# Two orders of one hand-written table of steps: packed attention and a gated feed-forward layer on one core

## The chip, the core and the metric

The kernel runs on one core of a Trainium2 chip. The metric is the device time of one execution in microseconds (us); lower is better. The time of the kernel before is the median of three runs.

## What is computed

Eight batches with eight heads each. In every head 32 "pack" queries `p` attend over 576 tokens, and the 576 queries `q` then attend over the 32 packed rows. The result goes through a layer with a sigmoid gate. All is float32.

```
p_packed = softmax(p k^T / 8) v          # 32 x 64 for each batch and head
x        = softmax(q p_packed^T / 8) p_packed
h = x @ w_in;  g = h * sigmoid(h);  out = g @ w_out      # 4608 x 512, 512 x 2048, 2048 x 512
```

## The kernel before

The packed rows are multiplied into `w_in` first (steps `pp`), so that the hidden layer of a batch is a product of the attention weights with these packs. Every product is made of three: each factor is split into an upper and a lower part (`..._hi`, `..._lo`), upper times upper, upper times lower, lower times upper.

The whole program is a table of 1627 steps, the string `ORDER` (from L56 on). The loop at L869 reads it from left to right and calls one function for each step; the scheduler of the framework is told (L801) to keep that order on TensorE (PE), VectorE (DVE), ScalarE (ACT) and SyncE (SP), which issues the transfers. So each of these engines executes its own instructions in the order of the table, and waits in place when the next one is not ready. GpSimd (POOL) is not in that list.

The names of the steps, with the engine that does the work:

- `k`, `q`, `v`, `wf`, `pf`, `S`, `x`, `rk`, `T`, `b`: transfers, issued by SP. `wf` n fetches a chunk of the weights (chunks 0 to 7 of 512 KB, 8 to 19 of 1024 KB).
- `ws` ACT, `wc`, `wz`, `wi` DVE, `wj` DVE or POOL, `wu` ACT, `wl` DVE: a chunk is brought into shape and split. `r` DVE, `R` POOL, `ru` ACT, `rl` DVE: sums of pairs of `w_out`.
- Attention of batch b: `as` scores (PE), `ac` copies, `am` maxima (DVE), `ax` exponentials (ACT), `at` transposes (DVE), `ay` (from batch 1 on sixteen small transfers, L363), `aa` packed rows (PE), `an` DVE, `ai` PE, `aj` DVE. Then for the queries `aS` (PE), `aT` two transposes (DVE), `aM`, `aN` DVE, `aX` ACT, `aD`, `aE`, `aV` DVE, `aH` ACT and `aL` DVE: upper and lower part of the attention weights.
- `pp` PE, `pu` ACT, `pl` DVE: packs.
- Batches 0 and 1, units u = 0 to 31: `h` hidden product (PE, L587), `g` three activations (ACT, L598 to L600), `l` lower part (DVE, L605), `o` second product (PE, L643). `h0.0` to `o3.1` are halves.
- From batch 2 on, units 36 to 139 in pairs: `B` (PE, L587), `G`, `N` ACT, `I` three sums (POOL, L619 to L621), `F` upper part (ACT, L633), `L` lower part (DVE, L637), `O` (PE, L643). Units 32 to 35 and so on are remainders with only `F`, `L`, `O`.
- `W` n: n products of the identity that nobody reads (L191). `E`, `Y`, `e`: results and sums leave the accumulators.

From batch 1 on, `as`, `aS`, `aa`, `ai`, `pp`, `h` and `B` all write into one pool of two buffers in the accumulator memory:

```
    ps_two = ent(tc.tile_pool(name="ps_two", bufs=2, space=PSUM))
```

so each of them waits until the step that reads the last but one of these products has done so. ACT needs another table for Exp (`ax`, `aX`) than for Silu (`g`, `G`, `N`); where the order of the table of steps goes from the one to the other, the program has an instruction that loads it.

Of the kernel before, what the change touches and what calls it, by code (L numbers as in the profile page):

```python
# [72 lines left out]
o22 g24 h26 x1 r5 R5 rk4 o23 e23.0 l24 e23.1 ru5 rl5 h25 g25 aM2.1 T3 l25 b1 o24 o25 r6 g26 l26 aS2.0 rk5 aT2.0 k3  # L73
pp10 v3 aM2.0 pu10 h27 pl10 g27 l27 R6 ru6 o26 aN2.1 rl6 rk6 h28 r7 g28 l28 aN2.0 aX2.0 aD2.0 h29 o27 o28 h30 aX2.1
aD2.1 T1 R7 g29 l29 aE2.1 g30 l30 ru7 o29 T4 h31 g31 rl7 T2 aE2.0 x3 l31 aV2.0 rk7 aH2.0 o30 o31 e31.0 Z0. F32 pp11
pp12 e31.1 Z1. L32 O32 pu11 F33 S37 L33 T5 pu12 pl11 F34 pf13 aV2.1 aH2.1 pl12 O33 as3.0 L34 aL2.1 aL2.0 as3.1 ac3.0
# [5 lines left out]
G48 G49 I48 pp16 aN3.1 N48 O47 F48 L48 pu16 aN3.0 pl16 aX3.1 k4 B51 aX3.0 aD3.0 I49 F49 L49 aE3.0 aV3.0 B50 G50 N50
N51 pf17 I50 S49 aH3.0 aD3.1 G51 aL3.0 O48 O49 F50 S50 S51 as4.0 ac4.0 pp17 pu17 I51 L50 pl17 as4.1 O50 B52 F51 L51
N52 S52 v4 ac4.1 aE3.1 am4 pf18 G52 I52 S53 B53 G53 B56 aV3.1 aH3.1 F52 L52 N53 S54 N56 O51 E2.1 I53 F53 q4 B54 S55
G54 L53 G56 I54 O52 N54 F54 B55 N55 L54 I56 G55 aL3.1 pp18 ax4.0 ax4.1 I55 S56 O53 O54 at4.0 B57 pu18 S59 at4.1 ay4.0
F55 pl18 L55 B58 O55 S57 F56 L56 O56 G57 I57 F57 L57 G58 N58 S58 ay4.1 N57 I58 F58 B59 G59 L58 N59 B60 N60 S60 B61 O57
# [828 lines left out]
```

## Time and profile before

| | us |
|---|---|
| median of 3 runs (lowest, highest) | 695.2 (695.13, 695.38) |
| the profiled execution | 696.58 |
| its span, from the first instruction to the last | 694.8 |
| PE busy in the span | 674.6 |
| DVE busy | 425.9 |
| ACT busy | 386.5 |

An engine's busy time is the time in which at least one of its instructions runs. Instructions on PE overlap, so a duration of one is longer than what it adds; what a step adds is read from runs of steps. Times of rows are counted from the start of the span.

### The profile page before, as it was taken

What the parts mean: (1) busy time and instruction counts of PE and PEld (TensorE: products, weight loads), DVE (VectorE), ACT (ScalarE), POOL (GpSimd) and SP (SyncE); (2) the same over time, 40 slices, a digit from 0 to 9 for tenths busy, and PEclk for the clock granted to TensorE, in tenths of its full rate; (3) what the DMA queues carried; (4) which work ended last, traced back from release to release, by engine and by line L of the source; (5) the groups of instructions that cost most, each with busy time, mean ns of one, the idle gap of its engine ahead of it and who ended that gap; (6) DMA issues with size and microseconds to landing.
All of it is one profiled execution on the core that took longest, in us unless ns stands there. A gap on an engine that the chain in (4) does not pass through costs nothing.

```text
span 694.8 us, 14721 instructions
## 1 busy us (share of the span) xinstructions
PE 674.6 (97%) x5958; PEld 593.1 (85%) x5958; DVE 425.9 (61%) x588; ACT 386.5 (56%) x641; POOL 232.4 (33%) x336
## 2 busy tenths in 40 slices
...
PEclk9899999999999999999999999999999999999999
...
GB/s 362 321 138 300 289 218 174 232 267 193 367 242 290 267 223 328 360 253 260 284 339 284 186 276 328 336 268 130 364 346 174 290 120 324 252 317 184 218 132 45
DMA packets 55107, 178.62 MB, mean 257 GB/s; under 512 B 21760, under 2 KB 25856, under 8 KB 47360
## 3 DMA queue, kind: packets, MB, share of 16 engines
...
## 4 chain that ended last, share of the span: by engine, by line
PE 77%; DVE 10%; ACT 4%; DMA 4%; SPq 2%; issue 2%; POOL 1%; ACTq 0%; DVEq 0%
PE ps_acc L643 46%; PE ps_two L587 24%; PE ps_two L284 5%; DMA win<-in_w_out 2%; PE ps_two L384 2%; DMA sums_of_w<-sums_of_w 2%; SPq L363 2%; DVE tm L420 1%; DVE g_lo L605 1%; DVE w_raw L249 1%; DVE w_raw L253 1%; DVE g_lo L637 1%; DVE wo_lo L277 1%; DVE o L785 1%; DVE win L261 0%
## 5 line engine op out<-in xcount | busy, mean ns | idle before, releaser
L637 DVE TENSOR_TENSOR g_lo<-g,g_hi 128x896 fp32r<-128x896 f32 x96 | 106.4, 1116 | 131.2 <-ACT g_hi L633 128.4
L643 PE MATMUL ps_acc<-wo_hi,g_hi 128*128 128x256 f32 (+1 forms) x576 | 185.1, 321 | 0.8 <-DVE o L785 0.8
L643 PE MATMUL ps_acc<-wo_hi,g_lo 128*128 128x256 f32 (+1 forms) x576 | 183.9, 319 | 2.0 <-DVE g_lo L605 2.0
L643 PE MATMUL ps_acc<-wo_lo,g_hi 128*128 128x256 f32 (+1 forms) x576 | 183.6, 319 | 0.0
L587 PE MATMUL ps_two<-a_hi,pw_hi 128*128 128x288 f32 x512 | 153.1, 299 | 1.5 <-DVE tm L420 1.5
L619 POOL TENSOR_TENSOR g<-g 128x128 f32<-128x128 f32 x96 | 56.4, 587 | 290.7 <-ACT g L609 290.6
L587 PE MATMUL ps_two<-a_lo,pw_hi 128*128 128x288 f32 x512 | 151.4, 296 | 0.0
L587 PE MATMUL ps_two<-a_hi,pw_lo 128*128 128x288 f32 x512 | 151.4, 296 | 0.0
L633 ACT CAST g_hi<-g 128x896 fp32r<-128x896 f32 x96 | 89.8, 940 | 76.7 <-POOL g L621 45.0
L643 PEld LDWEIGHTS ps_acc<-wo_hi,g_hi 128*128 128x128 f32 x576 | 108.4, 188 | 16.3 <-issue 5.6
L643 PEld LDWEIGHTS ps_acc<-wo_hi,g_lo 128*128 128x128 f32 x576 | 108.7, 189 | 12.4 <-DVE g_lo L605 4.3
L643 PE MATMUL ps_acc<-sums_of_w,g_hi 128*128 128x256 f32 x576 | 116.7, 284 | 0.3 <-DMA sums_of_w<-sums_of_w 0.3
L643 PEld LDWEIGHTS ps_acc<-wo_lo,g_hi 128*128 128x128 f32 x576 | 108.5, 188 | 7.1 <-DVE wo_lo L277 0.3
L587 PEld LDWEIGHTS ps_two<-a_hi,pw_hi 128*128 128x128 f32 x512 | 96.7, 189 | 14.4 <-PE ps_two L284 6.7
L587 PEld LDWEIGHTS ps_two<-a_lo,pw_hi 128*128 128x128 f32 x512 | 96.6, 189 | 0.8
L643 PEld LDWEIGHTS ps_acc<-sums_of_w,g_hi 128*128 128x128 f32 x576 | 89.1, 189 | 9.3 <-issue 7.8
L587 PEld LDWEIGHTS ps_two<-a_hi,pw_lo 128*128 128x128 f32 x512 | 96.6, 189 | 0.0
L643 PE MATMUL ps_acc<-sums_of_w,g_lo 128*128 128x256 f32 x288 | 81.2, 282 | 0.0
L620 POOL TENSOR_TENSOR g<-g 128x256 f32<-128x256 f32 x96 | 75.0, 783 | 6.6
L609 ACT ACTIVATE g<-ps_two 128x512 f32<-128x512 f32 x96 | 56.9, 597 | 33.4 <-DVE g_lo L637 16.9
L643 PEld LDWEIGHTS ps_acc<-sums_of_w,g_lo 128*128 128x128 f32 x288 | 54.6, 190 | 0.3 <-DVE g_lo L637 0.3
L621 POOL TENSOR_TENSOR g<-g 128x128 f32<-128x128 f32 x96 | 52.3, 546 | 6.6
(129 smaller groups left out, 798.9 us busy)
## 6 DMA issues: line engine op xcount, KB each, us to landing
...
```

Source lines behind the costliest of these rows:

```text
L249: nc.vector.tensor_scalar(up.bitcast(F32), up.bitcast(F32), TOP, -TOP, op0=ALU.min, op1=ALU.max)
L284: nc.tensor.matmul(bank(par)[NP * i : NP * i + NP], lhs(r, i), rhs(r, i), start=True, stop=True)
L363: nc.sync.dma_start(self.e1T[NP * at : NP * at + NP, : some.shape[1], i], some)
L384: nc.tensor.matmul(self.ps[NP * i : NP * i + NP, par * D : par * D + D], e, vs[:n, c, h * D : h * D + D], start=(c == 0), stop=(c == 4),)
L587: nc.tensor.matmul(bank, p[:, par, cols], a[:, par], start=(n == 0), stop=(n == len(todo) - 1))
L609: nc.scalar.activation(g[:, : 4 * P].rearrange("p (e s) -> p e s", e=2), made["h", u, None][..., :MAIN], AF.Silu)
L619: nc.gpsimd.tensor_tensor(x[:, 4], x[:, 0], x[:, 2], ALU.subtract)
L620: nc.gpsimd.tensor_tensor(x[:, 5:7], x[:, 0:5:4], one, ALU.subtract)
L621: nc.gpsimd.tensor_tensor(x[:, 7], x[:, 3], x[:, 6], ALU.add)
L633: nc.scalar.copy(both[0], g)
L637: nc.vector.tensor_tensor(g_lo, g, g_hi.bitcast(F32), ALU.subtract)
L643: nc.tensor.matmul(out, g[:, rows], w, start=(first and n == 0), stop=(last and n == 2), skip_group_check=True)
```

## The change

`ORDER` is replaced by another order of the same 1627 steps. Each step is in both as often as in the other, with the same numbers; functions, engines, buffers and sizes of transfers are the same. The instructions that load ACT's tables follow from the order: Exp and Silu alternate 41 times in the order before and 45 times in the order after (9 times each up to `g21`).

Shown are both orders up to step `l21`, and of the rest the lines with the products `aS` of batches 3 to 7 that other parts of this text speak of.

```diff
 ORDER = """
-W1 W5 wf0 ws0 wc0 wz0 W4 wi0 k0 as0.0 as0.1 am0.0 W6 W1 wf1 am0.1 ax0.0 at0.0 ax0.1 wj0 ar0 ay0.0 at0.1 ws1 wc1 wz1
-ay0.1 v0 wf2 q0 wi1 aa0 an0 ai0 aj0 wf5 wj1 pp0 wf3 ws2 wc2 wz2 wi2 wj2 pu0 pl0 aS0.0 W1 aC0.0 aS0.1 wu1 aB0.0 wl1 ws5
-aC0.1 W1 wf6 aM0.0 wc5 aB0.1 aN0.0 ws3 aM0.1 aX0.0 wc3 aD0.0 ws6 aN0.1 aX0.1 W7 aE0.0 aU0.0 pp1 aD0.1 wz3 wf7 aE0.1
-wf4 ws7 aU0.1 aH0.0 k1 wi3 wz5 aL0.0 wj3 ws4 pu1 wc4 wc6 wu3 pl1 wi5 v1 as1.0 aH0.1 aL0.1 ac1.0 as1.1 ac1.1 h0.0 g0.0
-wl3 wj5 wu5 wz4 am1 wi4 h0.1 g0.1 wl5 wj4 wf9 W13 ax1.0 h1.0 h1.1 ax1.1 wf8 l0.0 wc7 at1.0 l0.1 o0.1 g1.0 at1.1 pp2
-g1.1 wz7 wz6 l1.0 l1.1 o0.0 pu2 wi6 pl2 h2.0 wi7 h2.1 wj6 ws8 wc8 o1.1 wj7 g2.0 l2.0 wu7 ws9 wf10 ar1 wz8 wl7 g2.1 pp3
-pu3 wi8 wc9 l2.1 ws10 o1.0 o2.0 o2.1 wz9 pl3 h3.0 wi9 wj8 g3.0 h3.1 g3.1 ay1 wf11 aa1 wj9 wc10 pp4 pu4 l3.0 o3.0 an1
-wz10 ai1 l3.1 wi10 pl4 aj1 ws11 wc11 wz11 wj10 o3.1 wu10 q1 h4 wl10 h5 g4 l4 aS1.0 wf12 aT1.0 aM1.0 aN1.0 o4 wi11 g5
-aS1.1 aT1.1 h6 l5 aX1.0 aD1.0 ws12 wc12 aE1.0 aV1.0 k2 h7 v2 g6 l6 aM1.1 wf13 aN1.1 wj11 wu11 wl11 wf14 o5 g7 l7 as2.0
-aX1.1 pp5 aD1.1 aE1.1 x0 aH1.0 aL1.0 o6 aV1.1 pu5 pl5 ac2.0 aH1.1 o7 e7.0 aL1.1 e7.1 h8 g8 h9 ws13 wz12 wi12 h10 l8 o8
-wj12 r0 R0 wc13 g9 l9 as2.1 ws14 wz13 ac2.1 am2 o9 g10 l10 h11 ru0 rl0 wf15 ws15 pp6 q2 r1 g11 o10 l11 R1 pu6 pl6
-ax2.0 ax2.1 o11 wc15 wi13 wj13 wz15 h12 g12 wi15 l12 rk0 T0 at2.0 wc14 ru1 rl1 h13 g13 h14 l13 wz14 wi14 wj15 wu15
-wf17 wl15 o12 wj14 o13 rk1 ws17 wc17 wz17 wf16 pp7 g14 l14 at2.1 pu7 pl7 r2 wu14 h15 o14 g15 l15 wl14 ws16 h16 o15 h17
-wc16 g16 ay2 e15.0 wz16 wi16 wj16 l16 e15.1 wi17 wj17 h18 o16 g17 l17 g18 R2 ru2 l18 h19 rl2 o17 pp8 g19 r3 aa2 wf18
-o18 rk2 ar2 an2 l19 x2 pu8 wf19 ws18 pl8 h20 R3 wc18 wz18 wi18 ru3 o19 g20 l20 ai2 aj2 h21 wj18 rl3 h22 wu18 rk3 wl18
-o20 g21 l21 ws19 r4 g22 wc19 b0 wz19 pp9 pu9 aS2.1 R4 ru4 wi19 pl9 o21 aT2.1 l22 h23 wj19 wu19 wl19 rl4 h24 g23 l23
...
-N47 O44 aS3.0 G47 I47 I46 pp15 pu15 aT3.0 aM3.0 pf16 F46 aS3.1 aT3.1 pl15 S47 L46 aM3.1 O45 F47 L47 B49 N49 B48 O46
...
-aS4.0 pp19 aT4.0 pu19 aM4.0 I62 F62 B63 G63 aN4.0 pf20 S64 O61 N63 pl19 I63 aS4.1 aT4.1 B65 aM4.1 S65 L62 F63 L63 G65
...
-I80 F80 L80 B82 S83 S82 N82 B83 I81 O80 F81 L81 N83 G82 aS5.0 G83 I83 pp23 pu23 aT5.0 aS5.1 I82 F82 aM5.0 O81 v6 F83
...
-pf27 E5.0 N98 G98 I98 O96 F97 aj6 aS6.0 aT6.0 aM6.0 L97 pp27 pu27 F98 pl27 B100 N100 aN6.0 aX6.0 O97 L98 G100 B99 S98
-O98 aD6.0 G99 S99 N99 B102 I99 F99 L99 B101 N102 I100 F100 L100 pf28 O99 aE6.0 aV6.0 G101 G102 N101 aS6.1 aT6.1 pp28
...
-F118 G119 aS7.0 aT7.0 aM7.0 S118 pp31 L118 aN7.0 pu31 B120 I119 N120 F119 G120 aX7.0 pl31 O118 I120 L119 B121 N121
-B122 F120 aD7.0 pf32 G121 N122 aE7.0 aV7.0 O119 S120 L120 G122 aS7.1 pp32 pu32 aT7.1 S121 pl32 B123 O120 aH7.0 I122
...
+wf0 W6 wf1 ws0 wc0 ws1 W1 k0 as0.0 wz0 wc1 wz1 wi1 as0.1 am0.0 W1 wi0 wj0 am0.1 wf2 wf3 ax0.0 ws2 wc2 wf7 wz2 ax0.1
+ar0 v0 W5 at0.0 ay0.0 ws3 wc3 wz3 wi2 ws7 wi3 W4 at0.1 ay0.1 q0 wc7 wj1 wz7 aa0 an0 ai0 wi7 aj0 wj3 wu1 wl1 W1 pp0 wu3
+wj2 wl3 r0 aS0.0 aC0.0 pu0 aS0.1 pl0 aB0.0 aM0.0 aC0.1 wf4 pp1 pu1 pl1 aN0.0 aB0.1 aM0.1 wf5 ws5 wc5 wf8 W13 wj7 wu7
+wf6 W7 aN0.1 aX0.0 aD0.0 aX0.1 aD0.1 aE0.0 aU0.0 aE0.1 ws4 wc4 ws6 k1 wz5 wc6 q1 ws8 wi5 W1 aH0.0 aU0.1 aH0.1 wz6
+as1.0 ac1.0 aL0.0 as1.1 wi6 aL0.1 ac1.1 wz4 h0.0 g0.0 wj6 h0.1 g0.1 l0.0 wi4 l0.1 h1.0 wf9 wl7 am1 wj5 wj4 h1.1 wu5
+o0.0 g1.0 g1.1 wl5 ax1.0 ax1.1 o0.1 l1.0 wc8 l1.1 at1.0 at1.1 pp2 pu2 o1.1 pl2 o1.0 h2.0 wz8 v1 ws9 h2.1 g2.0 wc9 g2.1
+wi8 pp3 pu3 R0 ru0 l2.0 wz9 o2.0 pl3 l2.1 wf11 wi9 wf10 ws10 wj8 o2.1 wj9 h3.0 g3.0 h3.1 g3.1 pp4 pu4 wc10 l3.0 ay1
+o3.0 l3.1 wz10 o3.1 pl4 wi10 wf12 h4 ws11 g4 ar1 wc11 wz11 aa1 an1 l4 ai1 aj1 wj10 wu10 h5 wl10 g5 aS1.0 aT1.0 o4 wi11
+aM1.0 aN1.0 aX1.0 aS1.1 aT1.1 aM1.1 aN1.1 pp5 pu5 wf13 l5 pl5 aD1.0 aE1.0 h6 o5 wj11 wu11 aX1.1 g6 k2 l6 h7 pp6 wl11
+o6 pu6 aV1.0 aD1.1 pl6 g7 aH1.0 aL1.0 ws12 l7 as2.1 wf14 as2.0 ac2.0 aE1.1 aV1.1 aH1.1 ac2.1 o7 e7.0 aL1.1 h8 rl0 rk0
+g8 l8 wc12 e7.1 am2 ws13 h9 v2 g9 h10 o8 l9 wz12 ax2.0 g10 wi12 wj12 wc13 l10 r1 wz13 h11 wi13 x1 o9 ax2.1 at2.0 g11
+l11 o10 ar2 wf15 h12 wj13 ws14 h14 at2.1 g12 l12 wc14 o11 h13 wz14 o12 x0 ws15 wi14 g13 wc15 l13 o13 wz15 R1 ru1 wf16
+rl1 g14 l14 ws16 pp7 ay2 wj14 wu14 wi15 h15 r2 o14 pu7 pl7 wc16 g15 l15 wj15 rk1 wu15 wl15 wl14 h16 g16 wz16 wi16 wf17
+wj16 o15 h17 wf18 l16 e15.0 e15.1 aa2 R2 ru2 an2 rl2 rk2 o16 r3 g17 l17 ws17 h18 wc17 wz17 o17 wi17 h19 wj17 ws18 g18
+pp8 l18 wc18 g19 wz18 q2 wi18 o18 wf19 pu8 pl8 R3 ru3 l19 h20 ai2 wj18 aj2 wu18 rl3 rk3 wl18 g20 l20 ws19 wc19 b0 o19
+aS2.0 aS2.1 wz19 aT2.0 o20 wi19 aT2.1 r4 aM2.1 h21 g21 l21 wj19 wu19 h22 pp9 g22 l22 aM2.0 pu9 pl9 o21 h23 wl19 k3 R4
...
+aM3.1 aN3.1 aS3.0 F42 L42 O41 aX3.1 B44 N44 S42 O42 aT3.0 I43 F43 G44 I44 F44 L43 S45 S44 pf15 B45 G45 B47 N47 O43 k4
...
+B61 F59 N61 ai4 S59 S61 O58 S60 pf19 S62 L59 G61 I60 F60 B62 O59 N62 L60 E3.0 G62 O60 I61 F61 aj4 aS4.0 L61 I62 pp19
...
+aX5.0 F80 aS5.1 aT5.1 pp23 pu23 L80 S81 pf24 B82 N82 O79 pl23 G82 B83 S82 v6 E4.0 I81 F81 L81 O80 O81 G83 aM5.1 S83
...
+L97 S98 B99 N99 aa6 G99 an6 O96 I99 ai6 B100 N100 aj6 pp27 O97 F98 L98 S99 k7 pu27 G100 pl27 aS6.0 aT6.0 aM6.0 aS6.1
...
+G116 S116 O115 S117 aa7 S118 I116 E6.0 an7 F116 L117 L116 B118 G118 I118 N118 B119 N119 G119 ai7 aj7 O116 aS7.1 aT7.1
+aS7.0 aT7.0 O117 F118 L118 B120 N120 B121 O118 S119 I119 F119 L119 aM7.0 G120 I120 aN7.0 aX7.0 F120 L120 aD7.0 B122
...
```

## Rows read from the trace of the kernel before

**Rows 1.** The page: the span, busy time of each engine with its share and its instructions, and the granted clock of TensorE in 40 slices of the span (9 is full speed).

```profile
span 694.8 us, 14721 instructions
PE 674.6 (97%) x5958; PEld 593.1 (85%) x5958; DVE 425.9 (61%) x588; ACT 386.5 (56%) x641; POOL 232.4 (33%) x336
PEclk9899999999999999999999999999999999999999
```

**Rows 2.** Busy time of each engine in stretches of the span: from, to, length, busy us (instructions) of PE, PEld, DVE, ACT, POOL, then the granted clock, the share of the DMA engines and GB/s.

```profile
0.00:28.77 28.77, 19.68 (x261) 14.28 (x261) 19.83 (x42) 17.45 (x32) 2.93 (x8) 0.96 0.96 388
28.77:126.73 97.96, 94.61 (x723) 73.98 (x722) 90.90 (x126) 75.58 (x124) 26.01 (x19) 0.98 0.59 209
0.00:147.75 147.75, 135.25 (x1175) 105.20 (x1176) 127.61 (x188) 105.82 (x178) 34.10 (x31) 0.98 0.68 252
201.30:694.80 493.50, 486.05 (x4445) 445.87 (x4437) 259.16 (x352) 254.34 (x419) 182.02 (x288) 1.00 0.70 258
```

**Rows 3.** The timeline at five places: start, duration, engine, line, operation, and in brackets the idle time of the engine before it with what ended it. They are `aL0.0` on DVE, the first product of `h0.0`, `l16` on DVE, the third product of `o16`, the first product of `O32`.

```profile
28.02 0.75 DVE L522 TENSOR_TENSOR a_lo<-ps_acc,a_hi 128x576 fp32r<-128x576 f32 x1
...
31.15 0.61 PE L587 MATMUL ps_two<-a_hi,pw_hi 128*128 128x288 f32 x1
...
126.05 0.68 DVE L605 TENSOR_TENSOR g_lo<-g,g_hi 128x512 fp32r<-128x512 f32 x1
...
126.79 0.50 PE L643 MATMUL ps_acc<-wo_hi,g_lo 128*128 128x512 f32 x1 [0.47 <-DVE g_lo L605]
...
201.34 0.50 PE L643 MATMUL ps_acc<-wo_hi,g_hi 128*128 128x512 f32 x1
```

**Rows 4.** The chain that ended last, in order of time, merged: start, what it added, engine, line, instructions. They are two steps `h`; one `o`; a `pp` and an `aS`; an `aa`.

```profile
144.38 3.19 PE ps_two L587 x24
147.57 2.80 PE ps_acc L643 x12
150.37 1.50 PE ps_two L284 x32
...
488.64 1.66 PE ps_two L384 x80
```

**Rows 5.** Groups of instructions on DVE, 0 to 150 us, shapes apart: line, operation, names, shapes, count, busy us, mean ns of one, idle time before them.

```profile
L253 DVE SCALAR_TENSOR_TENSOR w_raw<-w_raw 128x1024 int32<-128x1024 int32 x8 | 10.2, 1272 | 0.1
L249 DVE TENSOR_SCALAR w_raw<-w_raw 128x1024 f32<-128x1024 f32 x9 | 9.2, 1019 | 0.8 <-ACT w_raw L245 0.8
L721 DVE TENSOR_TENSOR w_pair<-wo_hi,wo_lo 128x512 f32<-128x512 f32 x10 | 6.4, 683 | 0.1
L249 DVE TENSOR_SCALAR w_raw<-w_raw 128x512 f32<-128x512 f32 x4 | 1.7, 426 | 5.8 <-ACT w_raw L245 5.8
L420 DVE STREAM_TRANSPOSE tm<-ps_two 128x288 f32<-128x288 f32 x4 | 1.7, 458 | 0.6 <-PE ps_two L284 0.6
L468 DVE TENSOR_REDUCE mx<-tm 128x18 f32<-128x576 f32 x2 | 1.5, 747 | 0.0
L261 DVE TENSOR_SCALAR w_raw<-w_raw 128x1024 int32<-128x1024 int32 x2 | 1.4, 696 | 0.1
```

**Rows 6.** The timeline of ACT around `ru0`, and what DVE waited for behind that step's line, summed over 9 to 135 us: engine, line, what it waited for, us in total, times, longest.

```profile
92.51 1.05 ACT L734 CAST w_sums<-w_pair 128x1024 fp32r<-128x1024 f32 x1 [2.69 <-POOL w_pair L729]
...
DVE w_sums L738 <- ACT w_sums L734: 2.1, 2, 1.7
```

**Rows 7.** The timeline at `ay1` (SP, the first of its sixteen transfers) and at `aa1` (PE), and half of the transfers of that line between 39 and 53 us: count, KB each, median us from issue to landing.

```profile
39.83 2.45 SPq L363 DMA_DIRECT2D tm<-tm  x2
52.64 0.30 PE L384 MATMUL ps_two<-kvq_t,tm 128*32 128x64 f32 x2
...
tm<-tm SPq DMA_DIRECT2D x8, 40.0 KB, 1.9
```

**Rows 8.** Waits of PE over the span for the transposes of `aT` (us in total, times, longest), and one of them in the timeline (`aS3.0`, `pp15`, `aS3.1`).

```profile
PE ps_two L587 <- DVE tm L420: 1.5, 6, 0.2
PE ps_two L284 <- DVE tm L420: 0.5, 2, 0.2
...
259.78 0.72 PE L284 MATMUL ps_two<-kvq_t,ppT 64*32 64x288 f32 x16
260.29 1.06 PE L284 MATMUL ps_two<-w_quarter,ppT 64*32 64x512 f32 x16
261.60 0.72 PE L284 MATMUL ps_two<-kvq_t,ppT 64*32 64x288 f32 x16 [0.24 <-DVE tm L420]
```

**Rows 9.** The page's groups of the work between `B` and `O` of a pair: engine, operation, shapes, count, busy us, mean ns of one, idle time before them with what ended it.

```profile
L637 DVE TENSOR_TENSOR g_lo<-g,g_hi 128x896 fp32r<-128x896 f32 x96 | 106.4, 1116 | 131.2 <-ACT g_hi L633 128.4
L633 ACT CAST g_hi<-g 128x896 fp32r<-128x896 f32 x96 | 89.8, 940 | 76.7 <-POOL g L621 45.0
L620 POOL TENSOR_TENSOR g<-g 128x256 f32<-128x256 f32 x96 | 75.0, 783 | 6.6
L609 ACT ACTIVATE g<-ps_two 128x512 f32<-128x512 f32 x96 | 56.9, 597 | 33.4 <-DVE g_lo L637 16.9
```

**Rows 10.** The timeline of ACT at a load of its table.

```profile
96.64 1.00 ACT L550 CAST pw_hi<-ps_two 128x1024 fp32r<-128x1024 f32 x1
97.66 1.28 ACT L331 ACT_TABLE_LOAD   x1
98.95 0.78 ACT L331 ACTIVATE tm<-tm,nm 128x576 f32<-128x576 f32 x1
```

More of the change, by code (lines that the diff above doesn't have):

```diff
@@ L72 @@
-o20 g21 l21 ws19 r4 g22 wc19 b0 wz19 pp9 pu9 aS2.1 R4 ru4 wi19 pl9 o21 aT2.1 l22 h23 wj19 wu19 wl19 rl4 h24 g23 l23
[L73 to L76, printed above, removed]
@@ L82 @@
[L82 to L86, printed above, removed]
@@ new lines @@
+h24 o22 ru4 rl4 T3 g23 l23 pp10 o23 rk4 g24 aN2.1 aX2.1 h25 r5 l24 pu10 e23.0 pl10 e23.1 R5 ru5 rl5 rk5 g25 l25 aN2.0
+aX2.0 h26 o24 o25 T1 g26 h27 r6 l26 o26 h28 g27 l27 o27 aD2.0 R6 aE2.0 aV2.0 g28 l28 ru6 rl6 T4 h29 h30 r7 R7 b1 q3
+rk6 aH2.0 g29 o28 l29 o29 g30 l30 ru7 rl7 pp12 h31 g31 aD2.1 aE2.1 pu12 l31 pl12 x2 o30 o31 x3 rk7 Z0. F32 T2 T0 T6
+as3.0 aL2.0 ac3.0 e31.0 e31.1 pp11 Z1. pf13 as3.1 T5 L32 S38 T7 pu11 pl11 ac3.1 S39 F33 L33 O32 B36 N36 G36 B37 G37
+I37 aV2.1 aH2.1 am3 S37 O33 F34 N37 L34 aL2.1 pp13 ax3.0 I36 S36 F35 L35 pu13 pl13 pf14 ax3.1 O34 at3.0 at3.1 O35 B38
@@ new lines @@
+F36 L36 ay3.0 v3 F37 Y0 O36 G38 B40 N38 B39 ay3.1 N40 L37 I38 F38 G39 L38 I39 G40 O37 F39 O38 I40 N39 B41 S40 L39 G41
+pp14 O39 I41 F40 L40 N41 pu14 aa3 pl14 B42 ar3 F41 an3 N42 G42 L41 B43 N43 ai3 I42 O40 G43 S41 aj3 aS3.1 aT3.1 S43
+aM3.1 aN3.1 aS3.0 F42 L42 O41 aX3.1 B44 N44 S42 O42 aT3.0 I43 F43 G44 I44 F44 L43 S45 S44 pf15 B45 G45 B47 N47 O43 k4
+N45 S46 L44 I45 E2.0 F45 B46 L45 aM3.0 G47 O44 I47 G46 pp15 O45 I46 N46 F46 L46 pu15 S47 B48 N48 O46 pl15 pf16 v4 B49
+aN3.0 F47 L47 O47 aD3.1 S48 G48 aE3.1 aV3.1 G49 N49 S50 aX3.0 B51 aH3.1 B50 I48 aD3.0 F48 L48 I49 F49 N50 aL3.1 L49
```

65 lines of the change are left out of this document (33 added, 32 removed).

## The prediction

> **What bounds the kernel now.** I read the page first: PE is busy 674.6 us of a span of 694.8, and its granted clock is full nearly throughout [rows 1]. So a new order of the same work can win at most the 20 us in which PE waits, and what counts is where they lie. The waits of PE, the chain and the busy time by stretches answer that, and they show two different stages.
>
> Up to about 127 us DVE sets the pace. Between the end of `aL0.0` at 28.77 and the end of `l16` at 126.73 it works 90.90 of 97.96 us [rows 2, 3]. The first hidden product `h0.0` starts at 31.15, and `o16` stands still until `l16` is through: its third product starts at 126.79, while its first two (2.80/12 = 0.23 each [rows 4]) had run [rows 3]. I therefore count `o16` as begun at 126.8 - 0.5 = 126.3.
>
> After that PE sets the pace. From 201.30 on it is busy 486.05 of 493.50 us, DVE 259.16, ACT 254.34 [rows 2]. There only small repeated waits can be won or lost.
>
> So I use two sums: for DVE, the idle time so far plus the work in front of a step; for PE, the work in front of a step since `h0.0`. PE's products are the same set before `h0.0` in both orders, apart from `W`.
>
> **PE's work.** Two `h` add 3.19, an `o` 2.80, a `pp` and an `aS` 1.50, of which I give the `pp` 1.0 and an `aS` or `as` 0.5, an `aa` 1.66 [rows 4]. The halves take half, and the one-wide `pp2` and `pp3` 0.4. In the order before, `h0.0` to `o16` has 8 half and 15 whole `h` (30.3), 8 half and 12 whole `o` (44.8), `pp2` to `pp7` (4.8), `aa1` (1.7) and four `as` and `aS` (2.0): 83.6 us. `W13` stands there too, but nobody needs it. `o16` at 126.3 is thus 42.7 us later than this work alone. At `O32`, which starts at 201.34 [rows 3], the work is 156.9 (28 whole `h`, 28 `o`, nine whole `pp`, two `aa`, six `as` and `aS`), so the lag is 44.4: another 1.7 were lost over 73.3 us of work.
>
> **DVE's work.** In the order after, the step that PE reaches with the most DVE work in front of it is no longer `o16` but `o21`. Up to `l21` DVE worked 127.6 us before (it ends at about 147.8, 20.2 us of which were idle [rows 2]). The new order puts the same steps in front of `l21` and seven more: `wc19` 1.02, `wz19` 1.27, `wi19` 0.70, `aT2.0` and `aT2.1` 4 x 0.46, `aM2.1` 0.75 and the two sums of `r4` 2 x 0.68 [rows 5]. That is 6.9 us, 134.5 in all. PE's work in front of `o21`, counted as above, is 8 half and 19 whole `h` (36.7), 8 half and 17 whole `o` (58.8), `pp2` to `pp9` (6.8), `aa1`, `aa2` (3.3) and six `as` and `aS` (3.0): 108.6 us.
>
> **DVE's idle time in the new order** is the unknown of the sum. At the start DVE waits 5.8 us for the first chunk in both [rows 5], and 28.77 - 19.83 = 8.9 us up to `aL0.0` before [rows 2]. After, `wf1` goes out ahead of `k0`, so the first scores come about 1 us later; the order gives DVE `wc1`, `wz1`, `wi1` for that, and I walked the first 35 us step by step to 9.4. There `aL0.0` has ten more steps in front of it (chunk 7, `wl3`, `r0`, `pl1`, parts of chunks 4 to 6, 5.5 us) and ends near 34.7, and `h0.0` starts 3.5 us later than before. That costs nothing by itself, since the DVE work is done earlier than before.
>
> From `aL0.0` on DVE was idle 97.96 - 90.90 = 7.1 us up to `l16` and 20.2 - 8.9 - 7.1 = 4.2 more up to `l21` [rows 2]. One cause goes: `ru0` stood on ACT 2.69 us waiting for POOL, with `g11` queued behind it, and DVE lost 2.1 in that [rows 6]. In the order after, `r0` comes before `aL0.0` and `ru0` only after `pu3`, `r1` likewise long before `ru1`, so POOL is through when ACT asks. That leaves 5.0 as the low end, and 11.3 as the high end if nothing is won and all that lay in front of `l21` returns. What returns are hand-overs from PE to DVE and back, `an1`, `aT1`, `l8`, `pl7` as before, and now `aj2` in front of the bound. I take 7.0, nearer the low end, because I take the 4.2 between `l16` and `l21` for waits for a PE that was itself late.
>
> **The sum, first stage.** `l21` ends at 9.4 + 7.0 + 134.5 = 150.9, `o21` counts as begun at 150.4, 150.4 - 108.6 = 41.8 us behind its work. From there I let PE lose in proportion to what it lost before, 48.3/73.3 x 1.7 = 1.1. The lag at `O32` is then 42.9 against 44.4: 1.5 us won.
>
> **Second stage.** PE waited eight times for `aT`, 2.0 us together [rows 8]. The pattern is `aS`, `pp`, then another product into the two buffers: `pp15` takes 261.60 - 260.29 = 1.31 instead of 1.0 [rows 8]. From batch 3 on the order before has seven of them (after `aS3.0`, `aS4.0`, `aS5.0`, `aS6.0`, `aS6.1`, `aS7.0`, `aS7.1`), the order after two (`aS4.0`, `aS5.1`); elsewhere an `aa`, a second `aS` or an `O` stands between. Five times 0.3 is 1.5 us won. Against that, the way from `B` to `O` of a pair (0.60 on ACT, three sums on POOL, the widest 0.8, 0.94, 1.12: at most 5.1 [rows 9]) is covered by less than 5.8 us of PE work five times before and six times after, four of these close together (110, 111, 113, 114), where DVE also has batch 7. I charge 0.4. The four further loads of ACT's table add 5.1 us to ACT, all behind `g21`, hidden under PE since ACT is idle 239 us there [rows 2, 10]. Transfers are the same set, and I leave PE's waits for them as they were. The end, from `B139` on, has the same PE order.
>
> Altogether 1.5 + 1.1 = 2.6 us less. The profiled execution has 694.8 in its span and 1.8 around it; it was 1.4 above the median. On the median: 695.2 - 2.6 = **692.6**.
>
> **Rivals.** A change below 0.2% (1.4 us) is what a measurement of this kernel can't tell from none.
>
> *DVE starves as before.* The whole idle time of 11.3 returns. The place I would look at is ACT: `ws17` and `ws18` stand in front of `g18` and wait for `wf17` and `wf18`, which SP issues only after the sixteen transfers of `ay2`. For: ACT held DVE up in just this way at `ru0` [rows 6]. Against: by the walk both chunks land some 5 us before `l18` is due. 4.3 us more make 696.9. It decides from an idle time of 9.6 on; between 8.2 and 11.0 the result is within 0.2% of before, which is the rival "no change", about 695.
>
> *A wait at `aa1`.* Before, `ay1` goes out at 39.83 and `aa1` starts at 52.64, 12.8 later, its last transfer landing just then [rows 7]. After, `at1.1` ends near 45.1, which makes 57.9, and PE is at `aa1` near 59.1. 1.2 us of cover; every us beyond holds PE and batch 1 and passes on to `o21`. From 4.0 late on nothing is won, from 5.4 on it is slower; 6 us late gives 697.4.
>
> *The extra table loads count.* None hidden, 5.1 us: 697.7. The row speaks against more than that: a load takes 1.28, starts 0.02 after the end of what was before it and the next activation starts 0.01 after it [rows 10]. The Trainium skill ("ScalarE: Activation LUTs", What ACT_TABLE_LOAD costs) adds a drain of 1.38 us to each load, 2.66 in all; with that the four would be an estimated 10.6 us and the time 703.2. The rows show no such drain.
>
> *More is won.* An idle time of 5.0 and no price for the short covers: 2.4 better, 690.2.
>
> **Numbers.** Forecast 692.6 with a chance of 0.42 (own range 691.0 to 693.8), more won 0.10, no change 0.24, DVE starves 0.12, `aa1` 0.08, table loads 0.04. So faster 0.52, same 0.24, slower 0.24. The range goes from the best case, 689.9, to the starving DVE, 697.0.
>
> **What would show it.** Right: `h0.0` near 34.7; the last stop of PE for `g_lo` of L605 at `o21` and not at `o14` or `o16`, near 150.9; no wait of ACT for POOL at L734; DVE busy about 134.5 up to `l21`; `O32` 1.5 us earlier; two or three waits for `aT` instead of eight; 46 table loads. Wrong: `aa1` or `aS1` waiting for transfers of L363, ACT waiting for chunks 17 or 18, PE still at half clock well after `h0.0`, or new waits of `O` behind L637 around pairs 110 to 114.

## The result, and the profile after

The order after takes 699.1 us (median of 4 runs, 698.35 to 699.42) against 695.3 of before measured beside it (4 runs): ratio 1.0051, 95% interval 1.0034 to 1.0069. It is slower by 3.8 us; 692.6 was forecast, and 697.0 was the end of the range. The profiled execution takes 699.0, its span is 697.2. Since the profiled execution of before was 1.3 above its median, the two traces differ by 2.4 us only.

From the page of after: span, busy time, granted clock, and the group of `L`, which answers to the first row of [rows 9]:

```profile
span 697.2 us, 14725 instructions
PE 677.9 (97%) x5958; PEld 595.4 (85%) x5958; DVE 431.4 (62%) x588; ACT 391.6 (56%) x645; POOL 232.2 (33%) x336
PEclk8989999999999999999999999999999999999999
L637 DVE TENSOR_TENSOR g_lo<-g,g_hi 128x896 fp32r<-128x896 f32 x96 | 109.9, 1148 | 139.3 <-ACT g_hi L633 136.3
```

ACT has four instructions more than in [rows 1], the four loads. DVE is busy 5.5 us longer with the same 588 instructions; 3.5 of that are the 96 `L`, which last 1148 ns instead of 1116.

Busy time of after in stretches, columns as in [rows 2]: up to the end of `aL0.0`, up to the end of `l21`, and the second stage:

```profile
0.00:34.22 34.22, 24.74 (x290) 19.35 (x290) 26.27 (x53) 20.66 (x36) 8.06 (x14) 0.86 0.91 362
0.00:153.31 153.31, 140.94 (x1234) 110.59 (x1235) 138.10 (x197) 107.81 (x180) 36.04 (x34) 0.96 0.71 260
201.30:694.80 493.50, 488.97 (x4445) 445.49 (x4429) 261.82 (x351) 257.31 (x420) 183.86 (x288) 1.00 0.70 258
```

Up to `l21` DVE works 138.1 us, not 134.5, and idles 15.2, less than the 16.4 that I allowed. The work is the surprise, not the idle time.

The timeline of after at `aL0.0`, `h0.0`, `pp8`, `l21` and `O32`, answering to [rows 3]:

```profile
33.47 0.75 DVE L522 TENSOR_TENSOR a_lo<-ps_acc,a_hi 128x576 fp32r<-128x576 f32 x1
...
36.30 0.61 PE L587 MATMUL ps_two<-a_hi,pw_hi 128*128 128x288 f32 x1
...
136.04 1.09 PE L284 MATMUL ps_two<-win,ppT 64*32 64x512 f32 x16 [1.15 <-DVE win L265]
...
152.48 0.85 DVE L605 TENSOR_TENSOR g_lo<-g,g_hi 128x512 fp32r<-128x512 f32 x1
...
202.95 0.50 PE L643 MATMUL ps_acc<-wo_hi,g_hi 128*128 128x512 f32 x1
```

`h0.0` starts at 36.30, 5.15 later than before; the longest stop of PE behind it is `pp8`, 1.15 us for `wj17` of DVE; `O32` starts at 202.95 instead of 201.34. In between stands the first product of `h1.0`, in before and in after (`W13` lies ahead of it in before only):

```profile
36.73 0.38 PE L587 MATMUL ps_two<-a_hi,pw_hi 128*128 128x288 f32 x1
...
38.96 0.39 PE L587 MATMUL ps_two<-a_hi,pw_hi 128*128 128x288 f32 x1
```

To compare orders I use a **lag**: the start of a step less the PE work ahead of it since `h0.0`, each kind of step at its usual price in the trace of before (`h` 1.59, `o` 2.80, `O` 2.49, `pp` 1.02, `aS` 0.51, `aa` 1.66). By it before is at 43.7 at `O32` (my rounder prices gave 44.4) and after at 44.3: the first stage lost 0.6 where 1.5 was to be won. The other 1.0 of the 1.6 us between the two starts of `O32` is work: in the new order `as3.0` and `as3.1` stand ahead of it. From `O34` to `O143` the lag grows by 11.9 before and by 13.7 after: the second stage lost 1.9 where 1.1 was to be won.

Selected runs. "Start of h1.0" is a time in us, the next three columns are lags, "growth" is that from `O34` to `O143`, the last is the median time with that of before beside it (single times for the k runs). The runs f2, f3, g2, g3 and k1 to k4 leave out or replace part of the computation; they show what that part costs and are no kernels to use.

| run | start of h1.0 | o13 | o17 | O32 | growth | time (before) |
|---|---|---|---|---|---|---|
| before | 36.73 | 39.2 | 42.3 | 43.7 | 11.9 | 695.3 |
| after | 38.96 | 41.1 | 41.6 | 44.3 | 13.7 | 699.1 (695.3) |
| e1_first | 38.09 | 40.0 | 40.7 | 43.7 | 11.5 | 697.1 (695.4) |
| f1_warm | 37.95 | 40.1 | 40.7 | 43.7 | 13.7 | 697.9 (695.8) |
| f2_after_nosum | 37.51 | 39.5 | 39.8 | 41.1 | 13.7 | 695.9 (695.8) |
| f3_before_nosum | 36.64 | 39.0 | 39.4 | 40.4 | 11.5 | 693.1 (695.8) |
| g2_after_nopool | 35.40 | 36.8 | 37.2 | 38.5 | 14.4 | 695.5 (695.6) |
| g3_before_nopool | 35.96 | 38.3 | 38.5 | 39.5 | 11.5 | 692.4 (695.6) |
| h1_r0_early | 36.42 | 40.1 | 42.4 | 43.6 | 11.5 | 696.5 (695.6) |
| k1_after_notab | 38.24 | | | 43.7 | 10.9 | 695.6 (695.8) |
| k2_before_notab | 36.44 | | | 43.3 | 10.7 | 695.0 (695.8) |
| k3_after_noI | 38.14 | | | 43.9 | 11.2 | 696.1 (695.8) |
| k4_before_noI | 36.41 | | | 42.5 | 10.7 | 694.2 (695.8) |

### The profile page after: what moved, and what is told of

It is laid out like the page before. It is cut to its first block, busy times and chain, and to the rows that moved or that the text cites. A ratio compares the mean times of both kernels' runs of the same rounds, so it can differ in the third digit from the quotient of the medians.

```text
span 697.2 us, 14725 instructions
## 1 busy us (share of the span) xinstructions
PE 677.9 (97%) x5958; PEld 595.4 (85%) x5958; DVE 431.4 (62%) x588; ACT 391.6 (56%) x645; POOL 232.2 (33%) x336
## 5 line engine op out<-in xcount | busy, mean ns | idle before, releaser
L637 DVE TENSOR_TENSOR g_lo<-g,g_hi 128x896 fp32r<-128x896 f32 x96 | 109.9, 1148 | 139.3 <-ACT g_hi L633 136.3
L619 POOL TENSOR_TENSOR g<-g 128x128 f32<-128x128 f32 x96 | 52.7, 549 | 289.1 <-ACT g L609 270.0
L620 POOL TENSOR_TENSOR g<-g 128x256 f32<-128x256 f32 x96 | 73.3, 764 | 6.9
L621 POOL TENSOR_TENSOR g<-g 128x128 f32<-128x128 f32 x96 | 59.2, 617 | 6.9
L613 ACT ACTIVATE rest<-ps_two 128x64 f32<-128x64 f32 x96 | 20.7, 223 | 63.0 <-PE ps_two L587 62.7
```

The lines of the kernel that those rows point to most:

```text
L613: nc.scalar.activation(rest[:, 2 * p : 2 * p + 2, b % 2, hf], made["h", u, None][..., MAIN:HS], AF.Silu)
L619: nc.gpsimd.tensor_tensor(x[:, 4], x[:, 0], x[:, 2], ALU.subtract)
L620: nc.gpsimd.tensor_tensor(x[:, 5:7], x[:, 0:5:4], one, ALU.subtract)
L621: nc.gpsimd.tensor_tensor(x[:, 7], x[:, 3], x[:, 6], ALU.add)
L637: nc.vector.tensor_tensor(g_lo, g, g_hi.bitcast(F32), ALU.subtract)
```

## The experiments

### Which stage

The first run has the order after up to `O32`, and then what is left in the order before; at the seam:

```diff
 ac3.1 S39 F33 L33 O32
-B36 N36 G36 B37 G37 I37 aV2.1 aH2.1 am3 S37 O33 F34 N37
...
+v3 S37 F34 aV2.1 aH2.1 O33 L34 aL2.1 O34 B36 N36 G36 S36
...
```

> The order after up to and with O32, then the remaining steps in the order before. It leaves out nothing. Theory A (the loss of 3.8 us arises in the second stage, behind O32, where the trace of after shows the larger lag): within 1 us of the kernel before, 694.5 to 696.5, with O32 about 0.6 later than before. Theory B (it arises in the first stage, because DVE's work ahead of l21 became 3.6 us longer and PE stood behind wj17): 698 to 699.

Measured: 697.1 us, ratio 1.0025 (1.0014 to 1.0036), single runs from 695.9 to 698.4. So about 1.7 of the 3.8 us come from the first stage (1.0 to 2.5 by the interval), and what is left, 2.1, from the second: part in each. In the profiled execution the first stage of this run ends no later than that of before (lag 43.7 in both), and behind it the lag grows by 11.5; but that execution (695.9) was one of the two shortest of eight, so its trace shows less than the median lost.

The halves exchanged (the order before up to `O32`, then what is left in the order after):

> The order before up to and with O32, then the remaining steps in the order after. Theory A: 698 to 699, as slow as after. Theory B: within 1 us of before. Theory C (part in each stage): 696.5 to 698 here and the rest of the 3.8 us in the run with the halves exchanged.

Measured: 703.8. The seam costs by itself: at it the scores of batch 3 wait for a copy of ACT and `B36` for a late `pl12` of DVE, and PE loses 4.6 us in all ahead of `O33`, part of it because its granted clock stands at 0.50 from 209 to 212 us, and 1.3 more at `O36`. The time can't be used; from `O36` on the lag grows by 13.2, as in after (13.2).

The order after with one stretch, from `O57` to `O74` or to `O79`, in the order before; its beginning:

```diff
 F58 L58 S58 O57
-G60 ar4 ay4.1 aa4 an4 B61 F59 N61 ai4 S59 S61 O58 S60
...
+S59 ay4.1 S60 B61 O58 F59 L59 G60 I60 F60 L60 O59 N61
...
```

> The order after, but from O57 to O74 (about 320 to 390 us) with the steps in the order before. In the trace of after PE's lag grows there by 1.9 us, with B66 held 0.7 us by ACT, which loads its table for G64 only once B64 is through. If that stretch costs what the trace shows: 1.5 to 2 us faster than after, about 697. If the lag is only moved to another place: 698.5 to 699.5, as after.

> The order after, but from O57 to O79 with the steps in the order before; the transfers of ay5 now go out well ahead of aa5, so that the 10.7 us wait of the run before it does not return. In that run PE's lag from O58 to O74 grew by 1.97 as in before (1.96), against 3.81 in after. If this stretch is a cause of its own: about 1.8 us faster than after, 697.3. If what is saved is lost at the next waits: 698.5 to 699.5.

Measured: 707.7 and 701.3, both slower than after, again by seams. In the first, waits of PE between 395 and 413 us:

```profile
PE ps_two L384 <- DMA tm<-tm: 6.9, 3, 2.4
```

`aa5` stood for transfers of `ay5` that had just gone out. In the second PE lost 4.5 us between `O78` and `O80`, to the `aT` of batch 5 and to `G` behind products that the seam put close together. Inside the stretch itself both did what the order before does: from `O58` to `O78` the lag of the second grows by 2.45 (before 2.45, after 4.21). So this stretch holds 1.8 of the second stage's loss; by time alone that wasn't to be shown.

### The first stage: POOL holds DVE

In the trace of after, two instructions of `wl` that last 1.22 us elsewhere; first DVE, then POOL in the same microseconds:

```profile
115.36 1.23 DVE L553 TENSOR_TENSOR pw_lo<-ps_two,pw_hi 128x1024 fp32r<-128x1024 f32 x1 [0.63 <-ACT pw_hi L550]
...
117.66 1.22 DVE L605 TENSOR_TENSOR g_lo<-g,g_hi 128x512 fp32r<-128x512 f32 x1
118.80 1.76 DVE L277 TENSOR_TENSOR wo_lo<-w_raw,wo_hi 128x1024 fp32r<-128x1024 f32 x1
120.48 1.76 DVE L277 TENSOR_TENSOR wo_lo<-win,wo_hi 128x1024 fp32r<-128x1024 f32 x1
...
116.45 0.74 POOL L726 TENSOR_TENSOR w_pair<-w_pair 128x256 f32<-128x256 f32 x1
117.26 1.07 POOL L727 TENSOR_TENSOR w_pair<-w_pair 128x256 f32<-128x256 f32 x1
118.41 1.06 POOL L728 TENSOR_TENSOR w_pair<-w_pair 128x256 f32<-128x256 f32 x1
119.55 1.60 POOL L729 TENSOR_TENSOR w_pair<-w_pair 128x256 f32<-128x256 f32 x1
```

The `g_lo` of 1.22 is one that takes 0.68 [rows 3]. I took every DVE instruction that is over 0.1 us longer than its line and shape usually are: each of them overlaps one of POOL. Up to `l21` these excesses add up to 13.7 us in after (21 instructions) and 8.2 in before (14).

```diff
 def sums_of_pair(p):
+    if p < 5: return
```

> The order after, without the POOL sums of the pairs 0 to 4 (R0 to R4 do nothing, so these tiles keep plain copies). In the trace of after, every DVE instruction that lasts over 0.1 us longer than its kind usually does overlaps an instruction on POOL; up to l21 these excesses are 13.7 us, before 8.2. Theory A (these collisions make DVE late at wj17 and l21): the excess up to l21 falls by about 7.5, pp8 does not wait for wj17, O32 comes 2 to 3 earlier relative to h0.0, the time is about 696.5. Theory B (PE is late from the start, because h0.0 comes 5 us later): O32 follows h0.0 as before by about 8.0 of lag, time within 1 us of after.

> The order before, without the same POOL sums. R0 to R4 cause about 3.2 us of DVE's excess up to l21 here, and ru0's wait of ACT for POOL (2.1 on DVE) goes as well. Theory A: gains 2 to 3 us too, 692.5 to 693.5, and the first stage of after then ends no later than that of before. Theory B: gains as much, but O32 of after stays 1 to 2 later than that of before, since PE's lag at o13 was 41.1 against 39.2.

Measured: 695.9 (after it was 699.1) and 693.1. Both orders gain about 3 us, the excesses up to `l21` fall to 7.6 and 3.7, and `pp8` hardly waits. At `O32` after stays 0.7 behind before (0.6 with the sums). Neither expectation alone holds: POOL's sums do set DVE's pace, and they don't tell the orders apart, since half of the collisions of after (with POOL's joins) are still there. So these went too:

```diff
 def join(self, n):
+    if n in ON_POOL: return
```

> The order after with nothing on POOL up to l21: R0 to R4 and POOL's joins of the chunks (wj) are left out. No DVE instruction is then held by POOL there (13.7 us of excess in after). If the collisions are the one step in which my sum for the first stage failed: PE's lag at O32 is 1 to 2 us below that of the order before with the same parts left out, as forecast (1.5). If the late h0.0 or another part of the new order costs time by itself: it stays 0.5 us or more above it, as it did with the sums alone left out (41.1 against 40.4).

> The order before with the same POOL work left out; the partner of the run with the order after. It lost 8.2 us of DVE time to collisions up to l21, so it gains less from their absence than the order after. Collisions as the only cause: O32's lag here lies 1 to 2 us above the partner's. Otherwise 0.5 us or more below it.

DVE in the run with the order after, at the same two `wl`, and its busy time up to the end of `l21`:

```profile
113.31 1.22 DVE L277 TENSOR_TENSOR wo_lo<-w_raw,wo_hi 128x1024 fp32r<-128x1024 f32 x1 [0.43 <-ACT wo_hi L273]
114.46 1.22 DVE L277 TENSOR_TENSOR wo_lo<-win,wo_hi 128x1024 fp32r<-128x1024 f32 x1
...
0.00:146.51 146.51, 137.40 (x1225) 109.00 (x1233) 124.93 (x197) 107.25 (x180) 0.70 (x6) 0.98 0.73 269
```

and in the run with the order before:

```profile
0.00:143.96 143.96, 134.86 (x1175) 105.41 (x1176) 119.67 (x188) 105.12 (x178) 0.70 (x6) 0.98 0.69 259
```

Without POOL the same DVE work takes 124.9 instead of 138.1 us in after and 119.7 instead of 127.6 [rows 2] in before: the collisions cost 13.2 and about 8 of DVE's time. The excesses are gone, and in these two traces after is 1.0 ahead at `O32` (38.5 against 39.5), near the 1.5 of the forecast. That doesn't show that the collisions make the new first stage slower, for three reasons.

First, only half of them passes through: `l21` ends 6.8 us earlier in after (146.5) and 3.9 in before (144.0), and in the rest of that time DVE now waits for others. Second, after wins by a better beginning. Of the 5.8 us by which `O32` comes earlier (197.12), 3.6 are there at `h1.0`, and 2.3 are won behind it; in before 0.8 and 3.5. Ahead of `aL0.0` 1.5 us of collisions are gone and it comes 1.4 earlier, PE idles 1.63 instead of 2.33 us ahead of `aU0.0`, and its clock does not fall as it does in after (0.50, shown in the next part):

```profile
32.00:38.00 6.00, 5.57 (x60) 4.26 (x44) 6.00 (x12) 5.62 (x15) 0.00 (x0) 1.00 0.86 321
...
35.40 0.38 PE L587 MATMUL ps_two<-a_hi,pw_hi 128*128 128x288 f32 x1
...
197.12 0.50 PE L643 MATMUL ps_acc<-wo_hi,g_hi 128*128 128x512 f32 x1
```

Third, this execution was the shortest of ten (693.9). By median time the orders are 3.8 us apart with all of POOL's work, 2.8 without the sums and 3.1 without sums and joins (695.5 and 692.4). By the traces 2.9 lie in the second stage (14.4 against 11.5), 0.7 of them in one wait of PE for a transfer of `S` that isn't there in after. So POOL's work accounts for about 1 us of the difference by time at most, and the runs don't separate the collisions in it from the earlier start.

### The first stage: a late first hidden product

```diff
-aE0.0 aU0.0 aE0.1
+aE0.0 W10 aU0.0 aE0.1
```

> The order after with ten more products of W (W10) in the 2.3 us that PE idles ahead of aU0.0, so that the clock should stay at its upper level through aU0.1, as1.0, as1.1 and h0.0. If h0.0's lateness passes through (DVE stood idle 1.4 us at aL0.1 and ac1.1 for these products): h0.0 about 1 us earlier, O32 as much earlier, time about 698. If the lateness costs nothing by itself, as I had it: O32 unchanged, 699. If the clock falls anyway: nothing changes.

The stretch from 32 to 38 us, first after, then this run:

```profile
32.00:38.00 6.00, 6.00 (x48) 3.77 (x48) 5.01 (x10) 3.60 (x5) 1.42 (x1) 0.50 0.54 192
```

```profile
32.00:38.00 6.00, 5.38 (x59) 3.68 (x58) 6.00 (x12) 5.38 (x9) 1.42 (x1) 1.00 0.79 303
```

The granted clock is 1.00 (2.4 GHz) instead of 0.50 (1.2 GHz), DVE no longer idles, `h1.0` comes 1.0 earlier and `O32` 0.6. The time is 697.9, ratio 1.0027 (1.0017 to 1.0036): 1.2 less than after by the times, 1.7 by the two ratios to before. The lateness passes through, in this trace by 0.6 of 1.0. In the eight profiled executions of after's first stage with POOL at work, `h1.0` starts between 37.95 and 39.74, and `O32` always 163.8 to 164.4 us behind it. In the four with before's first stage as it is it follows 163.7 to 164.6 behind `h1.0` (36.4 to 37.2), with 1.0 less of work in between. So behind `h1.0` the new order is no slower than the old one: what its first stage loses, it has lost by `h1.0`. `h0.0` itself starts between 35.4 and 37.0 with this beginning (33.3 in the run without POOL), and at 30.8 to 31.2 with that of before, so the new order is late by an amount that changes from one execution to the next; I take this to be why e1_first spreads over 2.5 us.

The one part of the new order that was to save idle time of DVE, alone in the order before:

```diff
-o7 e7.0 aL1.1 e7.1 h8 g8 h9 ws13 wz12 wi12 h10 l8 o8 wj12 r0 R0 wc13
+r0 R0 o7 e7.0 aL1.1 e7.1 h8 g8 h9 ws13 wz12 wi12 h10 l8 o8 wj12 wc13
```

> The order before with r0 and R0 eleven steps earlier, ahead of o7: the one part of the new order by which ru0 no longer waits for POOL. In before ACT stood 2.69 us there and DVE 1.7 to 2.1. If that idle time is worth what my sum took it to be: O32 about 2 us earlier, time 693.3 to 694.5, faster than both kernels. If PE's products after it are held by something else anyway (wc14 and wc15 stretched by POOL at 105 and 111): under 0.7 us, 694.7 to 695.5.

Measured: 696.5, ratio 1.0012 (1.0003 to 1.0020). The wait at `ru0` is gone and nothing is won: at `o10` PE's lag is 40.0 instead of 39.1 and at `o15` 41.5 against 41.4. R0 now meets other DVE instructions, and the excesses up to `l21` are 9.7 instead of 8.2.

### The second stage: the loads of ACT's table

ACT in after around `aX4.0`, and the product `B66` of PE that waits for it:

```profile
341.80 1.28 ACT L488 ACT_TABLE_LOAD   x1
343.10 0.69 ACT L488 ACTIVATE tm<-tm 128x576 f32<-128x576 f32 x1
345.19 1.28 ACT L609 ACT_TABLE_LOAD   x1 [1.40 <-issue]
346.48 0.60 ACT L609 ACTIVATE g<-ps_two 128x512 f32<-128x512 f32 x1
346.98 0.22 ACT L613 ACTIVATE rest<-ps_two 128x64 f32<-128x64 f32 x1
347.08 0.94 ACT L633 CAST g_hi<-g 128x896 fp32r<-128x896 f32 x1
...
347.25 0.40 PE L587 MATMUL ps_two<-a_hi,pw_hi 128*128 128x288 f32 x1 [0.53 <-ACT rest L613]
```

ACT idles 1.40 us with the wrong table loaded, and loads the right one only when `B64` is through. `G64` and `N64` come 1.28 later for it, and so do `B66` (which needs their buffer) and `F63` behind them.

```diff
-aX4.0 aD4.0 O62 B64 G64 aM4.1 N64 F63 L63 B65
+O62 B64 G64 N64 F63 L63 aX4.0 aD4.0 aM4.1 B65
```

> The order after with one change: aX4.0 and aD4.0 stand behind N64, F63 and L63 instead of ahead of O62 B64 G64. In after ACT finishes this Exp at 343.79, stands 1.40 us for B64, and only then loads the table for G64 (345.19 to 346.47); B66 loses 0.70 and O63, O65 wait for their L. Theory: PE's lag from O62 to O65 grows by about 0.4 instead of 1.34, so O65 comes about 1 us earlier relative to O62, and it is still earlier at O80. Rival (the table load is not what holds them, ACT is late anyway or the wait moves to N65): the lag from O62 to O70 grows by 2.2 as in after. The time itself, 1 us of 699, is at the limit of what three rounds tell.

Measured: 700.1, and the rival holds: `B66` and `O63` no longer wait, but the next product, `B67`, does:

```profile
352.46 0.40 PE L587 MATMUL ps_two<-a_hi,pw_hi 128*128 128x288 f32 x1 [0.96 <-ACT g L609]
```

From `O62` to `O65` the lag grows by 1.44 (after 1.34), and to `O70` by 0.5 more than in after. Two loads and an Exp take 3.25 us of ACT wherever they stand among products that wait for ACT. So the loads were taken away altogether behind batch 2, in both activations that used Exp (L331, L488; these runs leave out the exponentials from batch 3 on):

```diff
-AF.Exp
+AF.Exp if self.b < 3 else AF.Silu
```

> The order after with Silu in place of Exp from batch 3 on, so that ACT loads no table behind g21 except for batch 2. The sums of the order are unchanged otherwise. If the loads are what the second stage lost: PE's lag from O34 to O143 grows by 11.5 or less instead of 13.7, and no more than with the order before treated alike. If not: it grows by over 13 here, or the two orders stay 1.9 apart.

> The order before with Silu in place of Exp from batch 3 on; the partner of the run with the order after. If the loads cost PE time in both orders, the lag from O34 to O143 falls below the 11.5 to 11.9 of before here too, by less than in after.

The first products of `O34` and of `O143`, in after, in the order after without the loads, and in the order before without them:

```profile
212.87 0.50 PE L643 MATMUL ps_acc<-wo_hi,g_hi 128*128 128x512 f32 x1
...
689.85 0.39 PE L643 MATMUL ps_acc<-wo_hi,g_hi 128*128 128x512 f32 x1
```

```profile
212.31 0.50 PE L643 MATMUL ps_acc<-wo_hi,g_hi 128*128 128x512 f32 x1
...
686.45 0.39 PE L643 MATMUL ps_acc<-wo_hi,g_hi 128*128 128x512 f32 x1
```

```profile
207.74 0.50 PE L643 MATMUL ps_acc<-wo_hi,g_hi 128*128 128x512 f32 x1
...
685.88 0.39 PE L643 MATMUL ps_acc<-wo_hi,g_hi 128*128 128x512 f32 x1
```

From 476.98 to 474.14 us in the order after: the loads cost 2.8. Set side by side step by step, the two traces of after part at five places: by 0.4 at `B38`, by about 1.1 from `B66` to `B67` (the load shown above), 0.3 at `O73`, 0.4 at `pp30` and 0.6 at `B115` and `O113`. In the order before the growth falls from between 11.5 and 11.9 (five executions) to 10.7: 0.8 to 1.2. Without loads the orders are 0.2 apart instead of about 2 (single executions). The longer `L` is not the cause: without loads it stays as long in after (before without them has 1117):

```profile
L637 DVE TENSOR_TENSOR g_lo<-g,g_hi 128x896 fp32r<-128x896 f32 x96 | 109.7, 1146 | 139.6 <-ACT g_hi L633 136.8
```

The other candidate:

```diff
 def pair_sums(u):
...
-    nc.gpsimd.tensor_tensor(x[:, 4], x[:, 0], x[:, 2], ALU.subtract)
-    nc.gpsimd.tensor_tensor(x[:, 5:7], x[:, 0:5:4], one, ALU.subtract)
-    nc.gpsimd.tensor_tensor(x[:, 7], x[:, 3], x[:, 6], ALU.add)
+    nc.gpsimd.memset(x[:, 4:8], 0.0)
```

> The order after with one memset on POOL in place of the three sums of each pair (I), which waits for nothing. The way from B to O is then shorter by 1.8 to 3 us, and POOL's instructions that hold DVE's L are gone. If this way is what the second stage lost: the lag from O34 to O143 grows by under 12 instead of 13.7, and is within 0.7 of the order before treated alike. If the tables or the two buffers are: the two orders stay 1.5 or more apart.

> The order before with the memset in place of the sums of each pair; the partner. Its lag from O34 to O143 grows by 10 to 11.5; its waits for aT (seven in this stage, 0.3 each) stay, so that the order after, which has two, would come out 1 to 1.5 lower if nothing else differed.

The growth is 11.2 and 10.7, 0.5 apart. Taking away either nearly closes the gap. Both lie in one chain, `B` `G` `I` `F` `L` `O`: a load makes PE wait only where the chain has no slack, and the sums on POOL are what uses it up. So the loads are what differs between the orders, and I take the length of that chain to be why they cost PE anything. Between `O34` and `O143` after has 32 loads and before 30; how much of the 2 us is the two more and how much the worse places isn't separated, but one place, `B66` and `B67`, holds 1.1.

### Can the causes be turned round

Three runs on the order before: the first two lines of the diff, the rest of it, both. In the rest, `r2` to `rk2` and `r3` to `rk3` are taken from their places and stand here:

```diff
-W7 aE0.0 aU0.0 pp1 aD0.1
+W7 W18 aE0.0 aU0.0 pp1 W5 aD0.1
...
-g18 R2 ru2 l18 h19 rl2 o17 pp8 g19 r3 aa2 wf18 o18 rk2 ar2 an2 l19 x2
+g18 l18 r2 R2 h19 o17 pp8 g19 aa2 wf18 o18 ar2 an2 l19 ru2 rl2 rk2 x2
 pu8 wf19 ws18 pl8
+r3 R3
...
```

> The order before with W18 ahead of aU0.0 and W5 ahead of aU0.1, in which PE idled 2.7 and 0.7 us. Its clock was at the lower level from 26.9 to 33.3, at as1.0, as1.1, h0.0 and h0.1. If an earlier h0.0 passes through here too: h1.0 and O32 about 1 us earlier, 694.3. If DVE's work up to l16 sets the pace, which does not start earlier by it: no change, 695.1 to 695.7.

> The order before with r2, R2, ru2, rl2 and rk2 some 15 us later (behind l18) and those of pair 3 some 6 us later. R2 held DVE by 2.1 us at 119 to 124, in its work ahead of l16, and r2 itself (1.4) goes from there. If the collisions and the work ahead of l16 set the pace: o17's lag 0.9 lower (41.4 instead of 42.3), O32 0.5 to 1 earlier, 694.5. If the sums collide as much where they stand now: no change.

> Both edits of the two runs before it. If they add up: 693.5 to 694.3, faster than both kernels. If one takes the place of the other: 694.3 to 695.

Measured: 695.4, ratio 0.9998 (0.9987 to 1.0009); 699.0, ratio 1.0053; 699.6. The first put in too many products: in the profiled execution (696.7) `h1.0` came 1.1 later, and `O32` only 0.5, so in the order before about half of such a delay is caught up. The second won 1.8 us at `o17` (lag 40.5 instead of 42.3), more than I had expected, and lost 4.5 behind it, because the sums of the next pairs were now late for ACT. Waits of ACT from 140 to 160 us:

```profile
ACT w_sums L734 <- POOL w_pair L729: 6.3, 2, 3.5
```

None of the runs beats both kernels with the whole computation. One with pair 2 late and the pairs behind it spaced out wasn't run.

## Why the prediction was wrong

The forecast missed by 6.5 us, about 3.2 in each stage by time.

**What held.** PE sets the pace of the second stage; that DVE sets that of the first held in part, as half of the work taken from DVE brought `l21` forward. DVE's idle time was sized well (15.2 against 16.4), ACT no longer waits for POOL at L734 up to `l21` (for POOL's joins it still does, 2.4 us in two waits at L273), the waits for `aT` fall from eight to three, 2.0 us [rows 8] to 1.0:

```profile
PE ps_two L587 <- DVE tm L420: 0.8, 2, 0.5
PE ps_two L284 <- DVE tm L420: 0.2, 1, 0.2
```

`aa1` didn't wait for transfers. ACT stood 2.2 us for chunk 18, and DVE was busy meanwhile, as the walk had it.

**First failed step: "134.5 us in all".** I added durations that DVE's instructions had in the order before to the busy time of the order before, as if a duration belonged to the instruction. Some 8 us of those 127.6 were POOL's, and in the new order POOL's share is 13.2, as the runs without POOL show. Own work rose by 5.3 (119.7 to 124.9), not 6.9; collisions rose by 5.2, for which the sum had nothing. Together 138.1, 3.6 over the forecast, and with 1.2 less idle time `l21` ends 2.4 later than forecast. In [rows 5] the sign was to be seen: `L249` of 128x1024 has a mean of 1019 ns; without POOL it takes 0.68 us. It is part of why the forecast gain of 1.5 did not come: PE stood 1.15 at `pp8` behind such work, and hardly without POOL's sums. That the first stage became slower than before goes back to the next step.

**Second: "That costs nothing by itself".** `h0.0` came 5.15 later, not 3.5. I had moved it with `aL0.0` to 34.7, but it stood 2.4 behind the end of `aL0.0` before as well [rows 3]. And DVE waits for these products: it idles 0.99 us at `aL0.1` and `ac1.1` in after, so its work is not "done earlier than before". At `h1.0` the new order was still 2.2 late; from there to `O32` both orders take equally long, so the delay arrives at `O32`: it starts 1.6 later, and by lag 0.6, since the new order has done 1.0 more of work by then. The sign "`O32` 1.5 us earlier" also forgot the two `as` that stand ahead of `O32` in the new order only: by my own sum it was to come 0.5 earlier.

**Third: the last stop at `o21`.** The bound was met earlier, at `pp8` for `wj17` (1.15 us). DVE's work up to a step that a `pp` waits for belongs among the candidates; I had looked at `o` alone.

**Fourth: the loads "hidden under PE since ACT is idle 239 us there".** A share over a stage said nothing of the place. This is most of what the second stage lost. The rival was on the list with a chance of 0.04 and a price of 5.1 us; the runs give 1.6 to 2.0 (2.8 in after less 0.8 to 1.2 in before). The rate of the Trainium skill ("ScalarE: Activation LUTs", What ACT_TABLE_LOAD costs), which adds a drain to each load, does not show in after either: an activation whose data are there starts 0.01 us behind a load.

**The term "1.5 won" for `aT`** was oversized: the waits themselves shrank by 1.0, and with the loads out the two orders grow by 10.9 and 10.7, so nothing of it is left in the end. The 0.4 for short covers can't be told apart from the loads.

**Open.** In the traces the first stage costs 0.6, by time 1.7. The profiled execution of before was 1.3 above its median: 0.4 of them lie in its second stage (11.9, where other traces of this order have 11.5), most of that in one wait of 0.3 for a transfer of `S`; where the rest lies isn't shown. Why `h0.0` of the new order moves by 1.6 us from one execution to the next isn't shown either.
